# Combination tiles of x in the superblocks, each at a place of its own modulo 128 bytes

## The chip, the core and the metric

The kernel runs on one core of one Trainium2 chip. The metric is the device time of one execution in microseconds. The matrix engine (TensorE, PE in the profile), VectorE (DVE), ScalarE (ACT) and GpSimd (POOL) work side by side; SyncE (SP) issues most transfers.

## What is computed

Chunked attention over q, k and v, then two gated feed-forward layers over 4608 tokens; the second one normalises its input rows first.

```python
x = np.ascontiguousarray(attn_out.transpose(0, 2, 1, 3)).reshape(B * S, H * D)   # 4608 x 512
def _moe_ref(x, w_gate, w_val, w_out):
    g = x @ w_gate                                    # 512 -> 1536
    silu = g * (1.0 / (1.0 + np.exp(-g)))
    val = x @ w_val
    return (silu * val @ w_out).astype(np.float32)    # 1536 -> 512
def _moe2_ref(x, w_gate, w_val, w_out, rms_g):
    rms = np.sqrt(np.mean(x * x, axis=-1, keepdims=True) + 1e-06)
    xn = x / rms * rms_g                              # and then as in _moe_ref, with weights of its own
```

## The kernel before

Every product is made of three single-pass fp32r matmuls on halves of the operands: high x high, high x low, low x high (`mm3`, lines 644 to 646). The first part of the program does the attention and the first layer for 2560 tokens in five blocks of 512. The second part, from about 574 us on, goes over seven *superblocks*: two finish the first layer for the last 2048 tokens, five do the second layer for all 4608. A superblock has two halves of tokens of `tw` columns (`SB`): 512 in the first five superblocks, 384 in the last two.

A superblock makes each product as a 2 x 2 product of blocks with seven multiplications in place of eight. For that the four blocks of x (`xf11`, `xf21`, `xf12`, `xf22`) are added and subtracted in place into seven *combinations*, k = 0 to 6. `x_prep` (lines 1025 to 1062) does it: `split` casts a combination on ScalarE to a high half (line 1041) and has VectorE subtract it from the source to get the low half (line 1042), `sub` forms the next combination (line 1046). The results are the *combination tiles* `xo{k}h` and `xo{k}l`, 1024 columns of 4 bytes in each of 128 partitions: two rows of 512 for the two halves of the contraction, `kt` 0 and 1. They live in the pool `X2`, which is opened at the right end of the memory late in the first layer (at block 4, step 8), where the pools of the attention and of the weights' preparation were.

In `gv_mm` (line 1067 on) the combination tiles are the moving operand. For each of 6 pairs of hidden chunks (`fp`), the products g and v and the combination k, six matmuls of `tw` columns add into one bank: `mm3` for `kt` 0 and 1. The stationary operand is one of the weight tiles `wrg`, `wrv`, loaded ahead through a ring of 16. `ORDER` puts the combinations in the order 0, 1, 4, 3, 5, 2, 6. The output product `y_mm` does the same with hidden tiles `hp` from another pool. Combinations of the next superblock are made during the output product of the present one (`XNEXT`); those of the first superblock during the last steps of the first layer (`XFIRST`, `XREST`).

The order of all instructions on all engines is written out by hand; the program only adds waits for data and for memory that is used again. A tile's place follows from the pool it is in and from the sizes of the tiles ahead of it. Line 1033 gives the last tile of the pool, `xo2l`, 16 columns more than it uses. In the layout that results all operands of the wide matmuls (512 or 384 columns), moving and stationary, lie 32 bytes past a multiple of 128. The tiles `w64`, `cr`, `cm`, `ws` and the identity `ident` lie at 0, the attention's `x`, `xq`, `xk`, `p` at 96; the stage tiles of the late weights (`lcr`, `lws`) lie at 32.

Of the kernel before, what the change touches and what calls it, by code (L numbers as in the profile page):

```python
# [10 lines left out]
F32R = mybir.dt.float32r  # L11
# [8 lines left out]
def tile_kernel(  # L20
# [24 lines left out]
    P = 128  # L45
# [135 lines left out]
    def chunk(j, f):  # L181
        return f if j % 2 == 0 else NF - 1 - f
# [638 lines left out]
    def score_at(i):  # L821
        return NP + 9 * (i - 8) // 2
# [6 lines left out]
    for i in range(NW // P, NT_):  # L829
        j = order[i] * P // NW  # L830
        if i >= 8:
            a = score_at(i)
# [14 lines left out]
        else:  # L847
            b = 9 * (i - 4)
# [69 lines left out]
    for j, p, nm in w1_at:  # L918
        a = 3 * min(chunk(j, 2 * p), chunk(j, 2 * p + 1)) + (3 if nm == "o" else 0)
# [88 lines left out]
    xo = {}  # L1008
# [16 lines left out]
    def x_prep(s, kt):  # L1025
        tw = SB[s][1]

        def tiles(k):
            if (s, k) not in xo:
                xo[s, k] = [  # L1030
                    X2.tile(
                        [P, 1024 + (16 if (k, z) == (2, "l") else 0)], F32R, tag=f"xo{k}{z}", name=f"xo{k}{z}_{s}"
                    )[:, :1024].rearrange("p (a b) -> p a b", a=2)
                    for z in "hl"
                ]
            return xo[s, k]

        def split(k, nm):
            h, l = tiles(k)
            x = xf[s, kt, nm]  # L1040
            nc.scalar.copy(h[:, kt, :tw], x[:, :tw])
            nc.vector.tensor_sub(l[:, kt, :tw], x[:, :tw], h[:, kt, :tw].bitcast(F32))

        def sub(o, a, b):
            o, a, b = (xf[s, kt, z][:, :tw] for z in (o, a, b))
            (nc.vector if s or kt else nc.gpsimd).tensor_sub(o, a, b)

        return {
            "0": lambda: split(0, "11"),
            "A": lambda: sub("11", "12", "11"),  # L1050
            "6": lambda: split(6, "22"),
            "B": lambda: sub("12", "22", "12"),
            "1": lambda: split(1, "21"),
            "C": lambda: sub("22", "22", "11"),
            "3": lambda: split(3, "11"),
            "D": lambda: sub("21", "21", "22"),
            "5": lambda: split(5, "12"),
            "4": lambda: split(4, "22"),
            "2": lambda: split(2, "21"),
        }  # L1060
# [650 lines left out]
```

## Time and profile before

| what | value |
|---|---|
| median of 2 runs | 1708.65 us (1708.29 to 1709.02) |
| the profiled execution's own time | 1709.08 us |
| its span, first to last instruction | 1707.3 us |
| PE matmul busy | 1685.3 us (99%) |
| VectorE, ScalarE, GpSimd busy | 1210.6, 865.9, 549.8 us |
| matmuls | 9870 |

The span is the time between the first and the last instruction on the core; the execution's own time has the launch around it. A matmul's duration in the profile reaches from its start to the modelled end of its last column's way through the array, so that durations of neighbours overlap; what it costs in a dense row is the distance from its start to the next one's start.

### The profile page before, as it was taken

What the parts mean: (1) busy time and instruction counts of PE and PEld (TensorE: products, weight loads), DVE (VectorE), ACT (ScalarE), POOL (GpSimd) and SP (SyncE); (2) the same over time, 40 slices, a digit from 0 to 9 for tenths busy, and PEclk for the clock granted to TensorE, in tenths of its full rate; (3) what the DMA queues carried; (4) which work ended last, traced back from release to release, by engine and by line L of the source; (5) the groups of instructions that cost most, each with busy time, mean ns of one, the idle gap of its engine ahead of it and who ended that gap; (6) DMA issues with size and microseconds to landing.
All of it is one profiled execution on the core that took longest, in us unless ns stands there. A gap on an engine that the chain in (4) does not pass through costs nothing.

```text
span 1707.3 us, 29702 instructions
## 1 busy us (share of the span) xinstructions
PE 1685.3 (99%) x9870; PEld 1428.5 (84%) x9870; DVE 1210.6 (71%) x1912; ACT 865.9 (51%) x2044; POOL 549.8 (32%) x581
## 2 busy tenths in 40 slices
PE   7999999999999999999999999999999999999998
PEld 5788888888788888878888888888888888999998
DVE  6996777888774887887987588734873477368356
ACT  6773554555443566655674455433543354344343
POOL 1005758678582366037813560000000000000000
PEclk9999999999999999999999999999999999999999
DMA  9997888998988688766887798876887678889986
GB/s 233 328 257 178 222 232 229 243 230 232 242 270 287 196 263 267 245 187 204 277 265 218 259 325 275 223 208 193 247 225 207 195 231 241 268 273 282 278 253 173
DMA packets 490904, 412.29 MB, mean 241 GB/s; under 512 B 280320, under 2 KB 369664, under 8 KB 490752
## 3 DMA queue, kind: packets, MB, share of 16 engines
q1 hardware_dynamic: 480576, 385.88, 78.2%
q0 software_dynamic: 6976, 24.12, 3.9%
q8 instruction: 79, 1.29, 0.3%
q10 hardware_dynamic: 3200, 0.39, 0.2%
q14 instruction: 73, 0.60, 0.1%
HBM read 325.06 MB, written 85.20 MB: 240 GB/s over the span
## 4 chain that ended last, share of the span: by engine, by line
PE 92%; DVE 4%; DMA 2%; ACT 1%; issue 1%; SPq 0%; POOL 0%; DVEq 0%
PE v L644 3%; PE g L646 3%; PE g L644 3%; PE g L645 3%; PE v L645 3%; PE v L646 3%; PE yvA L645 2%; PE ygA L645 2%; PE yvA L646 2%; PE ygA L644 2%; PE yvA L644 2%; PE ygA L646 2%; PE y L644 2%; PE y L645 2%; PE y L646 1%; PE y_b L646 1%
## 5 line engine op out<-in xcount | busy, mean ns | idle before, releaser
L1147 POOL TENSOR_TENSOR h<-h,h 128x512 f32<-128x512 f32 (+1 forms) x42 | 56.7, 1351 | 661.5 <-DVE h L1125 661.5
L1183 DVE TENSOR_TENSOR hp<-h,hp 128x512 fp32r<-128x512 f32 (+1 forms) x252 | 167.9, 691 | 23.7 <-ACT hp L1182 18.2
L1182 ACT CAST hp<-h 128x512 fp32r<-128x512 f32 (+1 forms) x252 | 140.6, 589 | 38.3 <-PE yvA L646 13.6
L1106 ACT ACTIVATE sgt<-sgt 128x512 f32<-128x512 f32 (+1 forms) x126 | 75.9, 602 | 162.2 <-DVE sgt L1113 162.1
L537 POOL TENSOR_TENSOR p<-p,r 128x512 f32<-128x512 f32 x36 | 41.2, 1146 | 194.2 <-DVE r L536 137.0
L1125 DVE TENSOR_TENSOR h<-h,sgt 128x512 f32<-128x512 f32 (+1 forms) x126 | 89.5, 710 | 16.2 <-ACT sgt L1106 3.9
L646 PE MATMUL g<-xh,l 128*128 128x512 f32 x240 | 94.3, 393 | 2.6 <-DMA l<-lo_scratch 2.6
L644 PE MATMUL v<-xh,wv 128*128 128x512 f32 x240 | 96.1, 400 | 0.7 <-ACT wo L168 0.7
L644 PE MATMUL g<-xh,wg 128*128 128x512 f32 x240 | 94.7, 395 | 1.6 <-ACT xh L618 1.0
L645 PE MATMUL g<-xl,wg 128*128 128x512 f32 x240 | 94.1, 392 | 0.4 <-DVE xl L638 0.4
L645 PE MATMUL v<-xl,wv 128*128 128x512 f32 x240 | 93.8, 391 | 0.0
L646 PE MATMUL v<-xh,l 128*128 128x512 f32 x240 | 93.7, 391 | 0.0
L656 ACT ACTIVATE sg<-g 128x512 f32<-128x512 f32 x60 | 35.8, 596 | 89.8 <-PE g L646 89.5
L657 DVE SCALAR_TENSOR_TENSOR sg<-sg,g 128x512 f32<-128x512 f32 x60 | 40.9, 681 | 43.6 <-ACT sg L656 43.2
L678 DVE TENSOR_TENSOR hl<-sg,hh 128x512 fp32r<-128x512 f32 x60 | 61.7, 1029 | 9.3 <-ACT hh L676 8.6
L509 ACT ACTIVATE p<-both,m 128x64 f32<-128x64 f32 x224 | 66.7, 324 | 1.1
L676 ACT CAST hh<-sg 128x512 fp32r<-128x512 f32 x60 | 37.1, 618 | 54.8 <-DVE sg L673 54.8
L644 PE MATMUL ygA<-hp,wro 128*128 128x512 f32 (+1 forms) x168 | 62.9, 374 | 0.2 <-ACT s3g L1099 0.2
L645 PE MATMUL ygA<-hp,wro 128*128 128x512 f32 (+1 forms) x168 | 62.9, 374 | 0.2 <-DVE hp L1183 0.2
L646 PE MATMUL yvA<-hp,wro 128*128 128x512 f32 (+1 forms) x168 | 62.8, 374 | 0.0
L646 PE MATMUL ygA<-hp,wro 128*128 128x512 f32 (+1 forms) x168 | 62.8, 374 | 0.0
L644 PE MATMUL yvA<-hp,wro 128*128 128x512 f32 (+1 forms) x168 | 62.7, 373 | 0.0
(851 smaller groups left out, 5509.1 us busy)
## 6 DMA issues: line engine op xcount, KB each, us to landing
wrg<-w_scratch SPq DMA_DIRECT2D x210, 256.0 KB, 3.2
wrv<-w_scratch SPq DMA_DIRECT2D x210, 256.0 KB, 3.1
wro<-w_scratch SPq DMA_DIRECT2D x210, 256.0 KB, 3.4
l<-lo_scratch SPq DMA_DIRECT2D x36, 512.0 KB, 5.4
wrg<-w_scratch SPq DMA_DIRECT2D x84, 128.0 KB, 2.9
wrv<-w_scratch SPq DMA_DIRECT2D x84, 128.0 KB, 3.0
wro<-w_scratch SPq DMA_DIRECT2D x84, 128.0 KB, 3.0
lo<-lo_scratch SPq DMA_DIRECT2D x40, 256.0 KB, 4.6
```

The costliest lines, as they stand in the source:

```text
L509: nc.scalar.activation(pt[:, hp, x], s3[:, x, hp], AF.Exp, scale=SCALE, bias=m[:, x, hp:hp + 1], accum_out=r[:, 2 * hp + x],)
L537: nc.gpsimd.tensor_tensor(out=p8, in0=p8, in1=r.to_broadcast([P, HP * 2, CH]), op=ALU.mult)
L644: nc.tensor.matmul(o, sh, mh, start=first, stop=False, skip_group_check=free)
L645: nc.tensor.matmul(o, sh, ml, start=False, stop=False, skip_group_check=free)
L646: nc.tensor.matmul(o, sl, mh, start=False, stop=last, skip_group_check=free)
L657: return sg, lambda: nc.vector.scalar_tensor_tensor(out=sg[:, :n], in0=sg[:, :n], scalar=1.0, in1=g[:, :n], op0=ALU.add, op1=ALU.mult)
L678: return product, lambda: nc.vector.tensor_sub(hl[:, :n], sg[:, :n], hh[:, :n].bitcast(F32))
L1106: nc.scalar.activation(t[:, :tw], src[:, :tw], AF.Silu)
L1125: nc.vector.tensor_mul(h[:, :tw], src[:, :tw], sgt[pos][:, :tw])
L1147: nc.gpsimd.tensor_sub(a, a, b)
L1182: nc.scalar.copy(hh[:, :tw], src)
L1183: nc.vector.tensor_sub(hl[:, :tw], src, hh[:, :tw].bitcast(F32))
```

## The change

Each combination tile is made 32 columns (128 bytes a partition) larger, `xo2l` as before 16 more, and the 1024 columns used begin `o` columns into it. High and low tile of a combination have the same `o`.

```diff
         def tiles(k):
             if (s, k) not in xo:
+                o = {0: 24, 1: 8, 6: 16, 3: 4, 4: 2, 5: 0, 2: 1}[k]
                 xo[s, k] = [
                     X2.tile(
-                        [P, 1024 + (16 if (k, z) == (2, "l") else 0)], F32R, tag=f"xo{k}{z}", name=f"xo{k}{z}_{s}"
-                    )[:, :1024].rearrange("p (a b) -> p a b", a=2)
+                        [P, 1024 + (48 if (k, z) == (2, "l") else 32)], F32R, tag=f"xo{k}{z}", name=f"xo{k}{z}_{s}"
+                    )[:, o:o + 1024].rearrange("p (a b) -> p a b", a=2)
                     for z in "hl"
                 ]
```

The layout that results, as the place of the first column used, in bytes past a multiple of 128:

| combination k | 0 | 1 | 4 | 3 | 5 | 2 | 6 |
|---|---|---|---|---|---|---|---|
| before | 32 | 32 | 32 | 32 | 32 | 32 | 32 |
| after | 0 | 64 | 40 | 48 | 32 | 36 | 96 |

All other tiles keep their place modulo 128. The other tiles of `X2` (`xf..`, `sgt..`) lie 1792 bytes lower than before. All engines have the same instructions in the same order. Only some waits on memory that was used before stand at another instruction, where the pool `X2` is opened. Most of them are on SP, at the first loads of x blocks (`xf_0_0` are the four of `kt` 0, `xf_0_1` those of `kt` 1; in brackets the semaphores waited for: `DMASW` transfers issued by GpSimd, `DMAHW` those of SP, `Pool` and `DVE` the engines):

```order
-L1022 DMA xf_0_0_6875<-x_scratch 128x512 [waits DMASW4_49,DMASW3_49,DMASW5_49,DMASW2_49,DMASW6_49,DMASW1_49,DMAHW5_49,DMASW0_49,Pool_49]
-L1022 DMA xf_0_0_6877<-x_scratch 128x512 [waits DMAHW6_49,DMASW0_49]
-L1022 DMA xf_0_0_6879<-x_scratch 128x512 [waits DMAHW7_49,DMASW6_49,DMASW4_49]
-L1022 DMA xf_0_0_6881<-x_scratch 128x512 [waits DMAHW0_49]
+L1022 DMA xf_0_0_6875<-x_scratch 128x512 [waits DMASW6_49,DMASW5_49,DMAHW5_49,DMASW4_49,DMASW0_49]
+L1022 DMA xf_0_0_6877<-x_scratch 128x512 [waits DMASW2_49,DMASW3_49,DMASW1_49,DMAHW6_49,DMASW0_49,Pool_49]
+L1022 DMA xf_0_0_6879<-x_scratch 128x512 [waits DMAHW7_49,DMASW0_49]
+L1022 DMA xf_0_0_6881<-x_scratch 128x512 [waits DMAHW0_49,DMASW6_49,DMASW4_49]
 L1022 DMA xf_0_1_6883<-x_scratch 128x512 [waits DMAHW1_49]
-L1022 DMA xf_0_1_6885<-x_scratch 128x512 [waits DMAHW2_49,DVE_49,Pool_49]
-L1022 DMA xf_0_1_6887<-x_scratch 128x512 [waits DMAHW3_49]
+L1022 DMA xf_0_1_6885<-x_scratch 128x512 [waits DMAHW2_49]
```

The wait for GpSimd goes from the first load to the second, and two of the transfers' waits go from the first to the fourth.

## Rows read from the trace of the kernel before

**Rows 1.** The page, parts 1 and 2: busy time by engine; granted clock by slice.
```profile
PE 1685.3 (99%) x9870; PEld 1428.5 (84%) x9870; DVE 1210.6 (71%) x1912; ACT 865.9 (51%) x2044; POOL 549.8 (32%) x581
...
PEclk9999999999999999999999999999999999999999
```

**Rows 2.** Timeline of PE, fifth and sixth chunk pair: start us, duration us, instruction.
```profile
1001.42 0.39 PE L644 MATMUL p4gA<-xo0h,wrg 128*128 128x512 f32 x1
1001.64 0.39 PE L645 MATMUL p4gA<-xo0l,wrg 128*128 128x512 f32 x1
...
1039.27 0.39 PE L646 MATMUL p5vC<-xo6h,wrv 128*128 128x512 f32 x1
1039.50 0.39 PE L644 MATMUL ygA<-hp,wro 128*128 128x512 f32 x1
```

**Rows 3.** Timeline of PE, first 384-column stretch of the last superblock.
```profile
1570.40 0.34 PE L644 MATMUL p0gA<-xo0h,wrg 128*128 128x384 f32 x1
1570.58 0.33 PE L645 MATMUL p0gA<-xo0l,wrg 128*128 128x384 f32 x1
...
1599.52 0.34 PE L644 MATMUL p2gA<-xo0h,wrg 128*128 128x384 f32 x1
```

**Rows 4.** Three stretches: length, busy time and count by engine, granted clock, DMA share, GB/s.
```profile
460.00:462.50 2.50, 2.50 (x8) 1.92 (x7) 0.00 (x0) 0.00 (x0) 0.70 (x1) 0.50 0.68 180
1000.00:1040.00 40.00, 40.00 (x178) 33.12 (x178) 31.70 (x44) 19.17 (x38) 14.50 (x13) 1.00 0.99 365
1390.00:1430.00 40.00, 40.00 (x178) 33.17 (x177) 37.38 (x65) 24.33 (x46) 0.00 (x0) 1.00 0.79 228
```

**Rows 5.** Instructions on tile xo0h: count, duration ns min/median/max, first and last start us.
```profile
L1041 ACT CAST xo0h<-xf x14: 507/614/616, 556.1 to 1552.2; 128x512 fp32r<-128x512 f32 x10, 128x384 fp32r<-128x384 f32 x4
L1042 DVE TENSOR_TENSOR xo0l<-xf,xo0h x14: 545/679/691, 556.8 to 1555.7; 128x512 fp32r<-128x512 f32 x10, 128x384 fp32r<-128x384 f32 x4
...
L644 PE MATMUL p0gA<-xo0h,wrg x14: 334/389/390, 573.7 to 1570.9; 128*128 128x512 f32 x10, 128*128 128x384 f32 x4
```

**Rows 6.** Chain of work that ended last, in order of time: start us, length us.
```profile
60.64 0.87 PE qkP L440 x8
85.47 0.87 PE qkP L440 x8
```

**Rows 7.** Timeline of PE, first layer, the half-clock stretch.
```profile
459.93 0.63 PE L644 MATMUL g<-xh,wg 128*128 128x512 f32 x1
...
462.49 0.63 PE L644 MATMUL v<-xh,wv 128*128 128x512 f32 x1
```

**Rows 8.** Timeline of PE, output product of a superblock.
```profile
1050.15 0.39 PE L646 MATMUL yvD<-hp,wro 128*128 128x512 f32 x1
...
1079.84 0.39 PE L645 MATMUL yvA<-hp,wro 128*128 128x512 f32 x1
```

**Rows 9.** Instructions of lines 243, 152, 612 and 618, columns as in rows 5.
```profile
L243 ACT CAST lwso<-lcro x42: 387/406/413, 778.0 to 1020.6; 128x256 fp32r<-128x256 f32 x42
...
L243 ACT CAST wsg<-wtg x24: 390/406/410, 186.3 to 419.7; 128x256 fp32r<-128x256 f32 x24
...
L152 DVE SCALAR_TENSOR_TENSOR crg<-crg,cmg x24: 673/691/3735, 23.2 to 394.8; 128x512 uint32<-128x512 uint32 x24
...
L152 DVE SCALAR_TENSOR_TENSOR lcro<-lcro x12: 676/690/1667, 773.4 to 1007.2; 128x512 uint32<-128x512 uint32 x12
...
L612 ACT COPY x<-both x16: 581/587/589, 222.7 to 538.4; 128x512 f32<-128x512 f32 x16
...
L618 ACT CAST xh<-both x12: 580/587/590, 167.9 to 414.0; 128x512 fp32r<-128x512 f32 x12
```

**Rows 10.** Timeline of SP's queue: start us, length us, issues.
```profile
542.72 4.04 SPq L1022 DMA_DIRECT2D xf<-x_scratch  x8
```

**Rows 11.** Instructions on tile wsv, columns as in rows 5, and its transfers' landing.
```profile
L256 POOL DMA_DIRECT2D w_scratch<-wsv x8: 537/578/597, 457.8 to 521.2; - x8
...
L249 POOL TENSOR_TENSOR wsv<-crv,wsv x6: 739/744/1245, 455.9 to 518.3; 128x256 fp32r<-128x256 f32 x6
...
DMA to landing us min/median/max: 3.4/5.3/6.8
```

**Rows 12.** Timeline of ACT, the first casts into a combination tile.
```profile
556.12 1.14 ACT L1041 CAST xo0h<-xf 128x512 fp32r<-128x512 f32 x2
```

## The prediction

> **What bounds the kernel now.** I read part 1 of the page first. TensorE's matmuls are busy 1685.3 us of a 1707.3 us span, and the granted clock is at nine tenths or more in all 40 slices [rows 1]. So the time is a count of matmuls times their spacing, and the first question is what one matmul takes where the changed tiles are read. That is read from start to start in the timeline, not from the mean duration in the cost groups: those durations overlap (389 ns each [rows 5], while a new one starts every 227 ns).
>
> The changed tiles are the moving operands of the gate and value products of all seven superblocks. From the start at 1001.42 to the one at 1039.50 there are 168 matmuls of 512 columns, 38.08 us, 226.67 ns each [rows 2]. From 1570.40 to 1599.52 there are again 168, of 384 columns, 29.12 us, 173.33 ns each [rows 3]. The difference, 53.34 ns for 128 columns, is 0.4167 ns a column, one column per cycle of the 2.4 GHz level. So 512 columns account for 213.33 ns and 384 for 160.00 ns, and 13.3 ns stay over per matmul at both widths. The change can act on those 13.3 ns, or add to them.
>
> The stage gives TensorE no idle time: 40.00 us of 40 in two stretches taken there, with 178 matmuls in each [rows 4]. ScalarE and GpSimd have much room, VectorE has little in the second stretch (37.38 of 40 us). So what another engine loses or wins is worth nothing here until VectorE falls behind.
>
> **The change part by part.** In the program's layout all moving and stationary operands of these products lie 32 bytes past a multiple of 128 today. Afterwards the seven pairs of combination tiles lie at 0 (k=0), 64 (k=1), 96 (k=6), 48 (k=3), 40 (k=4), 32 (k=5, as before) and 36 (k=2). No instruction is added, removed or moved; 1792 bytes a partition are taken. Three things could cost or gain.
>
> *The matmuls.* A combination has 6 pairs of chunks x 2 products x 3 matmuls for each of 14 half tiles [rows 5], 504 in all: 360 of 512 columns and 144 of 384. Per nanosecond and combination that is 0.504 us. The trace has no matmul of 512 or 384 columns whose moving operand starts elsewhere than at 32, so this price is bounded from both sides. Downward: the 13.3 ns vanish, at most 6.7 us a combination. The nearest row for that is the transposes, whose moving operand, the identity, starts at 0: eight take 0.87 us, 108.75 ns each [rows 6]. They are 128 columns, stream at 2 cycles a column (106.7 ns at 2.4 GHz), and keep 2.1 ns over, not 13.3. Taken over, that leaves 11.2 ns to win for a start at 0, 5.6 us a combination. Upward: a start that isn't a multiple of 8 bytes could need every fetch twice, 213.3 and 160.0 ns more, 99.8 us for one combination.
>
> I take nothing for all seven, for two reasons. In a stretch of the first layer in which half the clock was granted [rows 4], matmuls whose operands lie at 32 too start 427 ns apart (six steps in 2.56 us) [rows 7]; that is 512 columns at 1.2 GHz with nothing over. So the 13.3 ns are no cycles of the array. They fit a fixed time on the way of the operands, which the slow array hides. And the transposes take two cycles a column, so they would hide it too; their 2.1 ns are weak evidence on a start at 0. The output product, with hidden tiles at 32 in another pool, shows 226.6 ns as well (131 steps in 29.69 us) [rows 8].
>
> The Trainium skill speaks for a gain here. Its page "TensorE: Matmul & The Clock Gate", section "Wait — 56ns, not 53.3ns?", gives a warm matmul its columns at 2.4 GHz plus about 2.5 ns. The transposes agree (2.1 ns), these matmuls don't (13.3 ns). By that rule a place could at best give back 10.8 ns a matmul, an estimated 5.4 us for a combination, and by the trace nothing says that place is the reason.
>
> *ScalarE and VectorE.* They fill the tiles, 14 casts of 614 ns and 14 subtractions of 679 ns for each combination [rows 5]. The same cast takes 406 ns into tiles at 0 and 406 ns into tiles at 32. The same shift-and-or on VectorE takes 691 ns at 0 and 690 ns at 32, and a copy out of PSUM takes 587 ns to 96 and to 32 [rows 9]. So I cost them at nothing. If the subtractions at 48, 40 and 36 took twice their time, that would be 6 x 0.68 = 4.1 us a superblock on VectorE. Its idle 2.62 us of 40 [rows 4] would be used up first, and the remaining 1.5 us might reach TensorE, seven times 1.5 or 10 us at most.
>
> *The loads.* The pool grows downward over other dead tiles, so the first load inherits fewer waits and the second more; GpSimd's last product comes before the second load instead of the first. Eight loads leave SP in one run of 4.04 us from 542.72 us [rows 10]. What they newly wait for had ended: GpSimd's last subtraction of that kind starts at 518.3 us and takes 1.25 us at most, its last store is issued at 521.2 us, and such a store lands in 6.8 us at most [rows 11]. The first cast follows at 556.12 us, the first matmul on it at 573.7 us [rows 5, 12]. If the cover were gone, each microsecond of lateness would still have more than ten to spare. Nothing.
>
> The sum is 1709.08 (the profiled execution's own time, a span of 1707.3 and 1.8 around it) + 0. The median of the runs shown is 0.4 us lower, so I put 1708.7.
>
> **The rivals.** *A. Aligned starts are faster.* 13.33 ns is the time of 32 columns, and 32 columns are 128 bytes. A row of 2048 bytes that starts at 32 touches 17 pieces of 128 bytes: 17 x 32 x 0.4167 = 226.67 ns; one of 1536 bytes touches 13: 173.33 ns. Both are measured to the digit. If whole pieces are paid, only k=0 wins a piece, 5.6 us by the transposes' remainder: 1703.1. With pieces that make 64 as good as 0, k=1 wins too: 1697.5. Against it: a fixed time gives the same digits, and neither VectorE nor ScalarE cares for the place.
>
> *B. Operands at different places don't collide.* If the 13.3 ns come of moving and stationary operand at the same place modulo 128, six combinations win 11.2 ns each: 6 x 5.6 = 33.9 us, 1674.8. For it: the transposes mix 0 and 32. Against it: at half clock nothing is over.
>
> *C. Odd starts cost a little.* If a start that is no multiple of 16 bytes costs another 13.3 ns, k=2 alone adds 6.7 us (1715.4), k=2 and k=4 add 13.4 us (1722.1), and k=3 with them 20.2 us.
>
> *D. A start at 4 bytes breaks the stream, the case on the other side.* k=2 starts 36 bytes past the boundary, 4 past a multiple of 8. At one column per 2.4 GHz cycle the stream runs at 4 bytes every 0.4167 ns, and if it comes in pairs of columns, every pair of k=2 lies across two fetches. Doubled, that is +99.8 us: 1808.5; with one extra step for every fourth column a quarter of it, 1733.7. It decides from 68 ns a matmul of k=2 (34.2 us over 504). For it: such a start occurs nowhere in the wide matmuls. Against it: at half clock nothing is over, so the operands come faster than 512 columns in 426.7 ns need them; how much faster, no row shows.
>
> The skill has a rule that speaks against the change too: "SBUF — State Buffer", section "Specifications (TRN2)", has 16-byte lines and a penalty for each new one. Starts at 36 and 40 touch 129 lines instead of 128; with four columns a line that is an estimated 1.7 ns a matmul, 1.7 us for both. No row here shows such a penalty.
>
> **How the numbers follow.** Nothing changes: 0.52, 1707.5 to 1710. A: 0.22, 1697 to 1706. C, with a late VectorE: 0.10, 1711 to 1730. D: 0.12. B: 0.04. What a measurement can tell from no change is about 2%, 34 us. D lies beyond that in all but its mildest form, so slower 0.11; B lies at the edge, so faster 0.03; the rest is within, 0.86. The range runs from A with both aligned places (1697) to C with two odd starts (1722), which leaves out D, B and a little of C.
>
> **What would show it.** In the timeline of the changed kernel the spacing of the matmuls reads off each place by itself: 226.7 ns in all seven if I am right, about 215.5 on xo0 alone by A, 215.5 on all but xo5 by B, over 295 on xo2 by D. Spacing above 240 on any combination would make the prediction wrong, and so would idle time of TensorE put down to the subtractions of xo3, xo4 or xo2.

## The result, and the profile after

| | before | after |
|---|---|---|
| median | 1708.65 us | 1723.29 us (2 runs, 1722.78 and 1723.80) |
| ratio, 95% interval | | 1.0088 [1.0072, 1.0104] |
| span of the profiled execution | 1707.3 us | 1721.0 us |

The changed kernel is 0.9% slower: by less than the 2% that the prediction called the measurable bound, but clearly apart from no change. The forecast of 1708.7 us was wrong, and the time lies 1.3 us above the top of the range (1697 to 1722).

The page of the kernel after, parts 1 and 2: busy time by engine, and the granted clock by slice.

```profile
PE 1701.4 (99%) x9870; PEld 1431.1 (83%) x9870; DVE 1210.4 (70%) x1912; ACT 866.9 (50%) x2044; POOL 551.5 (32%) x581
...
PEclk9999999999999999999999999999999999999999
```

Against [rows 1], TensorE has the same 9870 matmuls and 16.1 us more of busy time. VectorE, ScalarE and GpSimd are within 2 us of what they had. The granted clock is as high. So matmuls start further apart, and the timeline says which. These are the first and the last of the 168 matmuls of 512 columns that answer to [rows 2], and of the 168 of 384 columns that answer to [rows 3] (start us, duration us, instruction).

```profile
1005.48 0.40 PE L644 MATMUL p4gA<-xo0h,wrg 128*128 128x512 f32 x1
1005.71 0.39 PE L645 MATMUL p4gA<-xo0l,wrg 128*128 128x512 f32 x1
...
1044.33 0.39 PE L646 MATMUL p5vC<-xo6h,wrv 128*128 128x512 f32 x1
1044.56 0.40 PE L644 MATMUL ygA<-hp,wro 128*128 128x512 f32 x1
```
```profile
1582.85 0.34 PE L644 MATMUL p0gA<-xo0h,wrg 128*128 128x384 f32 x1
...
1612.38 0.34 PE L644 MATMUL p2gA<-xo0h,wrg 128*128 128x384 f32 x1
```

39.08 us over 168 steps are 232.6 ns, where before had 226.67. 29.53 us over 168 are 175.8 ns, where before had 173.33. There are 15 stretches of the first kind and 6 of the second: 15 x 1.00 + 6 x 0.41 = 17.5 us lost. The output product, whose tiles were not moved, answers to [rows 8] and is as it was:

```profile
1049.82 0.39 PE L646 MATMUL yvA<-hp,wro 128*128 128x512 f32 x1
...
1079.51 0.39 PE L645 MATMUL yvA<-hp,wro 128*128 128x512 f32 x1
```

That is again 131 steps in 29.69 us, 226.6 ns. Summed over both traces from start to start, the 3528 matmuls on combination tiles went from 747.7 to 763.5 us (+15.8: the 17.5 us lost, less 1.7 us of waits and slower steps that before had among them), those on `hp` from 374.7 to 375.0, and the first layer's on `xh` and `xl` from 340.2 to 337.7, of which some 1.6 us are the half-clock stretch of [rows 4, 7], which did not occur in this execution (eight matmuls, 427 ns apart instead of 227). Together that is +13.6 us of the 13.7 us by which the span grew.

The stage still has no idle TensorE. Two windows of the kernel after (length; busy time and count of PE, PEld, DVE, ACT, POOL; granted clock, DMA share, GB/s):

```profile
1005.00:1045.00 40.00, 40.00 (x173) 32.35 (x172) 31.43 (x43) 19.31 (x38) 13.82 (x13) 1.00 0.98 353
1395.00:1435.00 40.00, 40.00 (x178) 33.12 (x177) 36.29 (x63) 23.02 (x44) 1.68 (x1) 1.00 0.77 223
```

In the first of them 40 us now hold 173 matmuls where they held 178 [rows 4], at full clock. The second one lies in the output product and holds 178 as before.

Now the single combinations. One piece of the timeline after, in which `xo5` (place 32 modulo 128, as before) hands over to `xo2` (place 36):

```profile
1018.03 0.39 PE L644 MATMUL p4vA<-xo5h,wrv 128*128 128x512 f32 x1
1018.26 0.40 PE L645 MATMUL p4vA<-xo5l,wrv 128*128 128x512 f32 x1
1018.49 0.39 PE L646 MATMUL p4vA<-xo5h,wrv 128*128 128x512 f32 x1
1018.72 0.39 PE L644 MATMUL p4vA<-xo5h,wrv 128*128 128x512 f32 x1
1018.95 0.40 PE L645 MATMUL p4vA<-xo5l,wrv 128*128 128x512 f32 x1
1019.18 0.39 PE L646 MATMUL p4vA<-xo5h,wrv 128*128 128x512 f32 x1
1019.41 0.40 PE L644 MATMUL p4gA<-xo2h,wrg 128*128 128x512 f32 x1
...
1020.82 0.40 PE L644 MATMUL p4vA<-xo2h,wrv 128*128 128x512 f32 x1
1021.05 0.41 PE L645 MATMUL p4vA<-xo2l,wrv 128*128 128x512 f32 x1
1021.30 0.40 PE L646 MATMUL p4vA<-xo2h,wrv 128*128 128x512 f32 x1
```

Six matmuls of `xo5` take 1.38 us, the six of `xo2` behind them 1.41; before, six took 1.36. Mean spacing of the 512-column matmuls by combination, from the medians of their starts in the whole trace, in the order of the program:

| k | 0 | 1 | 4 | 3 | 5 | 2 | 6 |
|---|---|---|---|---|---|---|---|
| place modulo 128 | 0 | 64 | 40 | 48 | 32 | 36 | 96 |
| spacing, ns (before 226.7) | 233.2 | 233.3 | 234.2 | 230.8 | 229.1 | 236.1 | 231.6 |

All seven lose, the aligned ones too, and `xo5` loses without having changed its place modulo 128. It is no matter of 36 and 40, then.

### The profile page after: what moved, and what is told of

It is laid out like the page before. It is cut to its first block, busy times and chain, and to the rows that moved or that the text cites. A ratio compares the mean times of both kernels' runs of the same rounds, so it can differ in the third digit from the quotient of the medians.

```text
span 1721.0 us, 29703 instructions
## 1 busy us (share of the span) xinstructions
PE 1701.4 (99%) x9870; PEld 1431.1 (83%) x9870; DVE 1210.4 (70%) x1912; ACT 866.9 (50%) x2044; POOL 551.5 (32%) x581
## 4 chain that ended last, share of the span: by engine, by line
PE 94%; DVE 3%; DMA 1%; SPq 1%; issue 0%; ACT 0%; POOL 0%; DVEq 0%; POOLq 0%
PE v L644 3%; PE g L644 3%; PE g L646 3%; PE g L645 3%; PE v L646 3%; PE v L645 3%; PE ygA L645 2%; PE ygA L646 2%; PE yvA L646 2%; PE ygA L644 2%; PE yvA L645 2%; PE yvA L644 2%; PE y L644 2%; PE y L646 1%; PE y L645 1%; PE y_b L646 1%
## 5 line engine op out<-in xcount | busy, mean ns | idle before, releaser
L1184 DVE TENSOR_TENSOR hp<-h,hp 128x512 fp32r<-128x512 f32 (+1 forms) x252 | 166.0, 683 | 24.4 <-ACT hp L1183 18.7
```

The costliest lines, as they stand in the source:

```text
L1184: nc.vector.tensor_sub(hl[:, :tw], src, hh[:, :tw].bitcast(F32))
```

## The experiments

Two theories stood after this. *Steps*: what counts is the distance from one moving operand to the next (high tile to low tile, 4096 bytes before, 4224 after). *Places*: what counts is the place of the moving operand modulo 128, against the weights or by itself. Four kernels ran first, together.

**Matmuls alone, over places and steps.** A kernel that leaves out all of the computation and runs nothing but matmuls on two big tiles, `m` moving and `w` stationary, which lie at equal places (both at 128 modulo 256). It runs 92 short sequences, each with its own starts `x` and `y` in bytes:

```
for name, n, seq in PLANS:
    ...
    for x, y, z in seq:
        nc.tensor.matmul(bank[z][:, :n], w[:, y // 4:y // 4 + 128], m[:, x // 4:x // 4 + n], ...)
```

> A kernel of matmuls alone: it copies q to the output and leaves the whole computation out. 92 plans of 12 to 16 matmuls each (single-pass fp32r, 128 x 128 by 512 columns, some narrower) follow each other without a wait; in each plan one thing is varied: the place of the moving operand, the place of the weights, the step from one moving operand's start to the next one's, or the number of columns. The theory of places (each start modulo 128 bytes has its own spacing): plans that repeat one moving operand show a spacing that changes with its place, 227 ns at 32 and 231 to 241 ns at other places, and a step from one place to another shows no more than the mean of the two. The rival theory of steps (what counts is how far the next matmul's start lies from this one's): plans that repeat one operand show 226.7 ns (512 columns) or 173.3 ns (384) at every place, and plans with a step show other values, from about 216 ns for a suitable step up to 241 ns, different for a step forward and back.

Both theories were off (mean spacing from the ninth matmul on). One moving operand at the weights' place, read over and over, goes at 226.7 ns. The same operand read over and over 32 bytes further on goes at 233.3, though its step is zero: steps alone don't explain it. At 128 bytes further on it goes at 230.3, though that is the same place modulo 128. At 256 and 512 it comes back to 226.7, and so do alternating operands that are 1024, 1536, 2048 or 8192 bytes apart, while 4224 and 2080 apart give 230.8 and 230.0. Moving the weights alone by 32, 64 or 128 slows them too (233.7, 234.3, 234.7). Some of these short sequences had not settled at the ninth matmul: 1024 bytes further on reads 230.7, and operands 256, 512 or 4096 apart read 228.6 to 229.0, with the last step at 226 or 227. So longer ones follow below.

**The larger tiles alone.**

```diff
-                o = {0: 24, 1: 8, 6: 16, 3: 4, 4: 2, 5: 0, 2: 1}[k]
+                o = 0
```
(against the kernel after)

> The changed kernel with o = 0 for every combination: tiles as large as in the change, but each starting at 32 bytes past a multiple of 128 as before, so that high and low tile are 4224 bytes apart instead of 4096. Theory of places: the place is as before, so 226.7 ns a matmul and 1708.7 us. Theory of steps: all combinations show what xo5 shows in the changed kernel, 1375 ns for six matmuls in place of 1360 (512 columns) and 1053 in place of 1040 (384), so 84 sixes x (5 x 15 + 2 x 13) ns = 8.5 us more, about 1717 us.

Measured: 1719.82 us, 1.0070 [1.0053, 1.0087]. The sizes alone, with every tile at its old place modulo 128, make most of the loss. Steps had said about 1717, places no loss.

**All starts at a multiple of 128.**

```diff
+                o = 24
```
(in place of the table)

> The changed kernel with o = 24 for every combination: all tiles start at a multiple of 128 bytes, 4224 bytes apart. Theory of places: all show what xo0 shows in the changed kernel, 1399 ns for six matmuls of 512 columns and 1054 for six of 384, so 84 x (5 x 39 + 2 x 14) ns = 18.7 us more, about 1727 us. Theory of steps: the steps are those of the kernel with pads alone, so the same time as that one, about 1717 us.

Measured: 1726.03 us, 1.0106 [1.0091, 1.0121]. That is what places had said, and not the 1717 of steps. Aligned starts are the worse, not the better:

```profile
1005.59 0.40 PE L644 MATMUL p4gA<-xo0h,wrg 128*128 128x512 f32 x1
...
1044.79 0.39 PE L644 MATMUL ygA<-hp,wro 128*128 128x512 f32 x1
```

39.20 us for the 168 matmuls, 233.3 ns each.

**All tiles 32 bytes lower, sizes as before.** The pool lies at the right end of the memory, so a larger last tile moves the whole pool.

```diff
-  [P, 1024 + (16 if (k, z) == (2, "l") else 0)]
+  [P, 1024 + (24 if (k, z) == (2, "l") else 0)]
```
(against the kernel before)

> The kernel before with 24 in place of 16 extra columns in the last tile and nothing else: the whole pool moves down by 32 bytes, all combination tiles and the blocks of x start at a multiple of 128, still 4096 bytes apart. Theory of places: about 1727 us, as every tile is at xo0's new place. Theory of steps: every step between starts is as before, so 226.7 ns a matmul and 1708.7 us.

Measured: 1721.06 us, 1.0081 [1.0066, 1.0096], a miss for both theories. The steps are those of before, so *steps* alone falls; *places* by its modulus of 128 had the sign right and the size wrong. In the timeline the spacing is 233.3 ns on the wide matmuls and 173.4 on the narrow ones:

```profile
1007.93 0.40 PE L644 MATMUL p4gA<-xo0h,wrg 128*128 128x512 f32 x1
...
1047.13 0.40 PE L644 MATMUL ygA<-hp,wro 128*128 128x512 f32 x1
```
```profile
1584.82 0.33 PE L644 MATMUL p0gA<-xo0h,wrg 128*128 128x384 f32 x1
...
1613.95 0.34 PE L644 MATMUL p2gA<-xo0h,wrg 128*128 128x384 f32 x1
```

**A third theory** fits all of this: what counts is the place of the moving operand *relative to the weights, modulo 256 bytes*. In the program's layout the weights of these products all lie at 160 modulo 256, and so did all combination tiles before: difference 0 everywhere. The new tiles are 4224 bytes long, which is 128 modulo 256, so high and low tile always differ by 128, and `o` shifts both by 4 `o`. After the change the differences are, high and low: `xo0` 96, 224; `xo1` 32, 160; `xo4` 8, 136; `xo3` 16, 144; `xo5` 0, 128; `xo2` 4, 132; `xo6` 64, 192. Only `xo5h` is where it was. The next four runs test this against the modulus of 128 and against a place by itself.

**Relative places, longer sequences.** The kernel of matmuls again, 75 sequences of 40 or 42.

> A kernel of matmuls alone (q is copied to the output, all else is left out): 75 plans of 40 or 42 matmuls. One sweep moves the moving operand by 4 to 512 bytes with the weights fixed, one moves the weights with the moving operand fixed, one moves both together, and some plans repeat the six matmuls of a combination (high, low, high, for two halves). Theory of relative place (the place of the moving operand against that of the weights, modulo 256 bytes, sets the spacing): 226.7 ns where the difference is 0 or a multiple of 256, in both sweeps alike, and wherever both move together; 229 to 237 ns elsewhere; six matmuls with low 4096 or 4352 bytes behind high 1360 ns, with 4224 bytes about 1375. Rival, absolute place modulo 128: the sweep of the moving operand returns to 226.7 ns at 128, the sweep of the weights shows 226.7 ns throughout, and moving both together shows 230 to 237 ns.

The page's timeline shows each sequence in one row (start us, from the first start to the last end us, name, count). Here the one with nothing moved, then moving operand +32, +128, +256, weights +32, +256, both +32, both +4:

```profile
34.98 9.23 PE L421 MATMUL caaa<-m,w 128*128 128x512 f32 x40
...
53.85 9.60 PE L421 MATMUL caac<-m,w 128*128 128x512 f32 x40
...
111.45 9.56 PE L421 MATMUL caai<-m,w 128*128 128x512 f32 x40
...
188.89 9.36 PE L421 MATMUL caaq<-m,w 128*128 128x512 f32 x40
...
332.58 9.60 PE L421 MATMUL cabf<-m,w 128*128 128x512 f32 x40
...
467.24 9.36 PE L421 MATMUL cabt<-m,w 128*128 128x512 f32 x40
...
543.86 9.34 PE L421 MATMUL cacb<-m,w 128*128 128x512 f32 x40
...
514.89 9.77 PE L421 MATMUL caby<-m,w 128*128 128x512 f32 x40
```

The first row reads (9.23 - 0.39) / 39 = 226.7 ns. The others hold one long first step after the change of sequence (some 110 ns more) and up to ten that settle, so the table takes the mean from the ninth start on, in ns:

| moved by, bytes | 4 | 16 | 32 | 64 | 96 | 128 | 160 | 192 | 224 | 256 | 512 |
|---|---|---|---|---|---|---|---|---|---|---|---|
| moving operand | 236.7 | 231.7 | 233.3 | 228.9 | 233.5 | 232.2 | 234.4 | 233.3 | 233.3 | 226.7 | 227.0 |
| weights | | 233.3 | 233.4 | 233.4 | 234.3 | 233.5 | 233.3 | 228.8 | 233.3 | 226.7 | 226.7 |
| both alike | 237.8 | 231.1 | 226.7 | 227.1 | 227.1 | 227.0 | 227.1 | 227.0 | 227.0 | | |

In steps of 32 bytes the rule holds: 226.7 to 227.1 where the two operands lie alike modulo 256 and 228.8 to 234.4 where they don't (the 227.1 are sequences in which the tenth and eleventh step still settle). Moving one operand up does nearly the same as moving the other one down: 228.9 for moving +64, 228.8 for weights +192 (that is -64); 234.4 for moving +160, 234.3 for weights +96; at 128 it is 232.2 and 233.5. Off the grid of 32 bytes the expectation failed: both at +4, +8 and +16 are slow although they lie alike (237.8, 231.1, 231.1), and the moving operand at +28 or +60 and the weights at +240 go at 226.7 although they don't. Triples of high, low, high go at 227.0 where the low tile lies 4096 or 4352 bytes from the high one, and at 232.1, 233.3 and 228.9 for 4160, 4224 and 4288; six at 4224 thus take 1400 ns, not the 1375 expected. With 384 columns the losses are smaller: 173.3 at +0, +64 and +224, 176.7 at +32 and +96, 176.0 at +128. The 173.3 at +224 is what the kernel with all tiles 32 bytes lower had shown.

**The whole pool 128 bytes lower.** Nothing changes modulo 128, neither place nor step.

```diff
-  [P, 1024 + (16 if (k, z) == (2, "l") else 0)]
+  [P, 1024 + (48 if (k, z) == (2, "l") else 0)]
```
(against the kernel before)

> The kernel before with 48 in place of 16 extra columns in the last tile: the whole pool moves down by 128 bytes; every tile keeps its place modulo 128 and its distance to the next. Relative place modulo 256: all combination tiles lie 128 off the weights, so the wide matmuls on them are slower, by 3 to 5 ns each as the short plans with a step of 128 showed (229 to 232 ns): 1715 to 1726 us. Place modulo 128 or steps alone: 1708 us.

Measured: 1726.96 us, 1.0101 [1.0081, 1.0122], 1 us above the range expected, with 39.04 us for the 168 matmuls, 232.4 ns each (the kernel of matmuls had 232.2 for +128):

```profile
1008.65 0.39 PE L644 MATMUL p4gA<-xo0h,wrg 128*128 128x512 f32 x1
...
1047.69 0.40 PE L644 MATMUL ygA<-hp,wro 128*128 128x512 f32 x1
```

The modulus of 128 falls.

**The changed kernel's tiles, brought back to difference 0.** Sizes, pool and waits as after; only the low tiles start 128 bytes in, the high ones at their beginning.

```diff
-                o = {0: 24, 1: 8, 6: 16, 3: 4, 4: 2, 5: 0, 2: 1}[k]
...
-                    )[:, o:o + 1024]
+                    )[:, (o := 32 if z == "l" else 0):o + 1024]
```
(against the kernel after)

> The kernel with pads alone, but with the low tile of each combination starting 32 columns (128 bytes) into its larger tile and the high tile at its start. All tiles lie 32 past a multiple of 128, as in the run with pads alone, but now low and high tile are 4352 bytes apart and all are at 160 past a multiple of 256, as the weights are. Relative place modulo 256: all of the loss is gone, 226.7 ns a matmul and 1708 us. Place modulo 128, or that larger tiles cost by themselves (1792 bytes, moved waits): 1720 us as with pads alone.

Measured: 1709.37 us, 1.0003 [0.9993, 1.0013]. The loss is gone:

```profile
1001.10 0.39 PE L644 MATMUL p4gA<-xo0h,wrg 128*128 128x512 f32 x1
...
1039.18 0.39 PE L644 MATMUL ygA<-hp,wro 128*128 128x512 f32 x1
```

38.08 us, 226.67 ns, as in [rows 2].

**Everything 64 bytes further on.** A small tile ahead of all, and none at the end of the pool: weights and combination tiles then all lie at 224 modulo 256.

```diff
+    const.tile([P, 16], F32, name="room")
...
-  [P, 1024 + (16 if (k, z) == (2, "l") else 0)]
+  [P, 1024 + 0]
```
(against the kernel before)

> The kernel before with one more tile of 64 bytes in the constants' pool and no extra columns in the last combination tile: nearly everything, moving operands and weights of all wide matmuls in both layers, moves up by 64 bytes to 96 past a multiple of 128. Relative place: differences are as before, so 226.7 ns and 1708 us. Absolute place (32 is a good place, others are not): all 7700 wide matmuls become slower by 5 to 8 ns, 1745 to 1770 us.

Measured: 1709.13 us, 0.9998 [0.9989, 1.0007]; the 168 matmuls take 38.08 us again. There are 7452 wide matmuls with both operands moved, not 7700. (The added line shifts the line numbers by one.)

```profile
1001.08 0.39 PE L645 MATMUL p4gA<-xo0h,wrg 128*128 128x512 f32 x1
...
1039.16 0.39 PE L645 MATMUL ygA<-hp,wro 128*128 128x512 f32 x1
```

160 modulo 256 before, 224 here and 128 in the kernels of matmuls all give 226.7 ns. On multiples of 32, a place by itself does not count, as long as both operands share it.

The five kernels in which all combinations have the same layout agree. Over all 3528 matmuls on combination tiles, without the few steps that hold a wait (16 ns or more above the floor of 226.67 or 173.33), they take 11.7 us more than before (larger tiles alone), 18.7 (all at a multiple of 128), 16.5 (32 lower), 18.1 (128 lower) and 0.0 (low tiles 128 in), against medians that moved by 12.1, 18.3, 13.3, 17.1 and -0.5 us. The changed kernel takes 17.1 more, against 14.6.

One layout doesn't give one loss, though. With the larger tiles alone, two stretches of 168 matmuls in the first superblock take 39.20 us each (233.3 ns a matmul), and all six in the fourth and fifth take 38.45 us (228.9 ns). Here are the ends of one of each:

```profile
616.85 0.40 PE L644 MATMUL p2gA<-xo0h,wrg 128*128 128x512 f32 x1
...
656.05 0.40 PE L644 MATMUL p4gA<-xo0h,wrg 128*128 128x512 f32 x1
...
1315.03 0.39 PE L644 MATMUL p2gA<-xo0h,wrg 128*128 128x512 f32 x1
...
1353.48 0.39 PE L644 MATMUL p4gA<-xo0h,wrg 128*128 128x512 f32 x1
```

The tiles and their places are the same in both. Every one of the five superblocks of 512 columns starts at 229 ns, in steps of 227, 234 and 226. In the first three, a pair of matmuls on other weights comes in the second chunk pair (`ones`, for the sums of squares of the second layer). From that pair on the spacing there is 231 to 233 ns, up to the output product. The last two have no such pair and stay at 229. So what ran before counts as well: with a difference of places there is a loss, but its size has more than one value. That the pair is the trigger is read from the order in time only; no run leaves it out.

No faster layout turned up: in both kernels of matmuls no sequence of 512 or 384 columns has a mean below 226.6 or 173.3 ns from its ninth start on, so the kernel before has the least spacing that was found.

## Why the prediction was wrong

**The bound was read rightly.** The time is a count of matmuls times their spacing, TensorE has no idle time in the stage, and the other engines don't matter. Casts and subtractions are in the median as long as in [rows 5]. On the tiles at 0 and at 36 in the kernel after:

```profile
L1042 ACT CAST xo0h<-xf x14: 508/616/617, 553.8 to 1564.7; 128x512 fp32r<-128x512 f32 x10, 128x384 fp32r<-128x384 f32 x4
L1043 DVE TENSOR_TENSOR xo0l<-xf,xo0h x14: 545/680/693, 554.4 to 1568.1; 128x512 fp32r<-128x512 f32 x10, 128x384 fp32r<-128x384 f32 x4
```
```profile
L1042 ACT CAST xo2h<-xf x14: 511/618/624, 581.1 to 1578.8; 128x512 fp32r<-128x512 f32 x10, 128x384 fp32r<-128x384 f32 x4
L1043 DVE TENSOR_TENSOR xo2l<-xf,xo2h x14: 520/682/1526, 582.2 to 1581.1; 128x512 fp32r<-128x512 f32 x10, 128x384 fp32r<-128x384 f32 x4
```

ScalarE and VectorE at nothing, and the loads and their moved waits at nothing, were right: the casts and subtractions by these lines, the loads and waits because the kernel that keeps the larger tiles and all the moved waits, but restores the difference 0, stands at 1.0003 to before, with an interval that holds no change.

**The step that failed is "I take nothing for all seven".** It rested on the half-clock rows: since nothing is left over at 1.2 GHz, the 13.3 ns are no cycles of the array, hence a fixed time. What follows is only that the slow array hides them. That a part which is hidden at half clock is the same at every place does not follow, and it is not: at full clock 226.7 ns is what the best relative place gives, and the others give 2 to 10 ns more. The term that I set to 0 is 15.8 us on the combination tiles, and 14.6 us in the medians.

**The bounds asked the wrong question.** Both ends were worked out for the place of *one* operand modulo 128. What the runs show is the difference of *two* operands modulo 256. In the layout before, that difference is 0 for every matmul on combination and hidden tiles, and the table of places modulo 128 hid that the larger tiles throw the low tiles off by half of 256. `xo5`, "as before" in my list, lost 2.4 ns a matmul for that reason.

**A row for it was there.** Not all wide operands lay at 32, as I had put it: the weights `ones` lie at a multiple of 128 (128 modulo 256), with moving operands at 160. Their 18 matmuls of 512 columns come in nine pairs, and the trace of before shows a loss at each pair. One of them:

```profile
774.01 0.39 PE L645 MATMUL p1vD<-xo1l,wrv 128*128 128x512 f32 x1
...
776.28 0.40 PE L646 MATMUL p1gA<-xo4h,wrg 128*128 128x512 f32 x1
776.51 0.39 PE L1293 MATMUL tssq<-ts,ones 128*128 128x512 f32 x1
776.75 0.40 PE L1294 MATMUL tssq<-ts,ones 128*128 128x512 f32 x1
...
778.60 0.39 PE L645 MATMUL p1gC<-xo3l,wrg 128*128 128x512 f32 x1
```

The ten steps up to 776.28 take 2.27 us, the ten from there on 2.32: 235, 232, 234, 236, 224, 230, 236, 229, 233 and 231 ns, then 227 again. At all nine pairs ten steps take 2319 to 2321 ns, without a wait, where the ten before them take 2266 to 2268. So a difference of 32 bytes had a price in the rows of before, and it pointed upward; the prediction took its price from the transposes instead.

**The rivals.** B named the right pair, moving and stationary operand, and had the sign the wrong way round: equal places are the good case, and the six combinations that left them lost. A is refuted: with all high and low tiles at a multiple of 128 the time is 1726.03 us, and in the kernels of matmuls, where both operands start at a multiple of 128, 226.7 ns is still the least. For C the odd starts are the worst ones (236.1 at 36, 234.2 at 40), but only 2.8 and 0.9 ns above the 233.3 of the aligned `xo1`, not 13.3 above the rest. D did not occur: no median step of `xo2` is above 241 ns, far from 295. The penalty for a new 16-byte line that the Trainium skill has ("SBUF — State Buffer", section "Specifications (TRN2)"), an estimated 1.7 us here, would have to fall on 36 and 40 alone, and most of the loss fell elsewhere.

**The 13.3 ns.** They did not vanish at any place. In the first kernel of matmuls, with equal places, they stay over at 512, 384 and 320 columns alike (226.7, 173.3 and 146.7 ns), while 448 and 480 columns have 16.0 ns over (202.7 and 216.0). The 2.5 ns of the Trainium skill ("TensorE: Matmul & The Clock Gate", section "Wait — 56ns, not 53.3ns?") were not reached by any 512-column sequence here, all of which load weights for every matmul.

**What stays open** is the way in which the two operands meet. A rule of the Trainium skill would not have them meet: "TensorE: Matmul & The Clock Gate", section "Step-by-step: what each phase is for", gives the streamed operand and the weight load two independent read ports, so that loading the next weights takes no read bandwidth from the running matmul. Here moving the weights by 32 bytes, with the streamed operand left alone, takes the spacing from 226.7 to 233.4 ns, and the measurement decides; whether it happens at those ports no run shows. Where they meet was not tried; it would need matmuls without a weight load between them. Nor does the difference of places give the exact size of a loss: triples 4224 bytes apart go at 233.3 ns in the kernel of matmuls, while the larger tiles alone, with the same distance, go at 229 or 231 to 233 ns, depending on what ran before.

## What to carry to other kernels

Where TensorE is the bound and every matmul loads new weights, as these fp32r matmuls do, put moving and stationary operands at the same place modulo 256 bytes, on a multiple of 32, and look at tile sizes before anything else: one tile of 128 bytes more shifts everything behind it. Read the spacing from start to start by tile, since a duration of 0.39 us does not change visibly while 6 ns of 227 go lost. And a quantity that is the same in nearly every row of a profile is not shown to be harmless there. Look for the few rows in which it differs, here 18 of 9870 matmuls, before setting its term to nothing; and when a change moves it, the range has to reach to both sides.

## What the runs showed of the hardware

- The spacing of 512-column fp32r matmuls with a weight load each settles at 226.7 ns if moving operand and weights lie alike modulo 256 bytes on multiples of 32, and at 229 to 234 ns at the other multiples of 32. 384 columns go at 173.3 ns, or up to 176.7; there differences of 64 and 224 bytes cost nothing.
- Equal places do not help off the 32-byte grid: both operands at +4 go at 237.8 ns, at +8 and +16 at 231.1.
- The rule has exceptions below 32 bytes: the moving operand alone at +28 or +60, and the weights alone at +240, go at 226.7.
- After a change of place it takes up to eleven matmuls until the spacing has settled, ten at the `ones` pairs of before; where operands alternate, it repeats in a fixed pattern (227, 234, 226 ns on `xo5`).
- One layout can have two lasting spacings: 229 ns, and 231 to 233 ns after a pair of matmuls on other weights (the larger tiles alone).
